# Transposing k's column maxima and spreading them over the partitions: the tensor engine's transpose mode in place of float32 products with the identity

## The chip, the cores and the metric

The kernel runs on one core of a Trainium2 chip. The metric is the device time of one execution in microseconds. The kernel before takes 540.25 us (median of three runs, 539.28 to 540.41).

## What is computed

For batch 8, 8 heads, 576 positions and head width 64, a linear attention feeds a gated MLP over 512 channels. The part that the change touches is the softmax of k over the positions (`axis=2`), which takes the maximum of each of k's columns first. Cut from the reference:

```python
    k_s = k - np.max(k, axis=2, keepdims=True)
    k_s = np.exp(k_s)
    k_s = k_s / (np.sum(k_s, axis=2, keepdims=True) + 1e-09)
    kv = np.einsum('bhsd,bhse->bhde', k_s, v)
    return np.einsum('bhsd,bhde->bhse', q_s, kv).astype(np.float32)
    ...
    h = x @ w_in
    ...
    v_s = np.einsum('ts,bsd->btd', w_sg, v_n) + b_sg[None, :, None]
    gated = u * v_s
    return (x + gated @ w_out).astype(np.float32)
```

The MLP has a tanh GELU behind `w_in` and a layer norm over one half of its channels ahead of `w_sg`.

## The kernel before, in words

All 8 batch elements (b) go through one core. Work is written as small steps, and a table (`PLAN`, lines 28 to 125) says in which order the steps are recorded; each engine then runs its instructions in that order. PE's matmuls all stand at line 330 (the helper `mm`), the other engines' at line 142 (the class `InOrder`), so in the profile steps are told apart by the names of their tiles.

The large products (`hv_mm`, `hu_mm`, `sg_mm`, `out_mm`: x by `wi`, normed v by `ws`, the gate by `wo`) are each split into three products of a high and a low part in the reduced float32 form (fp32r), with 288 or 512 moving columns. In the attention, k, q and v of one half h of the heads (4 heads, 256 columns) are handled at once, so every k step runs 16 times (b, h). The k steps in their order:

- `load_k`: DMA of k into tile `kk` (128 partitions of positions, 5 x 256).
- `k_max` (DVE, tile `km`): maximum over the five position tiles; 128 partitions x 256 columns are left.
- `kt_mm` (PE, line 354): for each 128 columns a matmul with the 128x128 block of `km` as the weights and `eye`, the float32 identity, as the moving operand. The result in PSUM is the block transposed.
- `k_top` (DVE, tile `kt`): maximum along the free axis of the PSUM tile; one number for each column of k is left, one a partition.
- `kb_mm` (PE, line 364): the column of `kt` is read as the weights, repeated 128 times (`broadcast_to([P, P])`), and again multiplied with `eye`: every partition of the PSUM tile gets all 256 maxima.
- `k_sub` (DVE, writes `kk` from `kk` and the PSUM tile), `k_exp` (ACT), `kv_mm` (PE, float32, `vv,kk` in the profile), which sums over the positions.

`kt_mm`, `kb_mm`, `kv_mm` and `hv_mm` take turns on two one-bank PSUM tiles (`ps1`); the other products use three two-bank tiles (`ps2`). `kt_mm` and `kb_mm` stand in PLAN among the large products, so that k's steps run beside them. A float32 matmul of the program becomes two weight loads and two matmuls in the profile (`eye,km` x64 for 16 `kt_mm` of two calls); an fp32r one becomes one of each.

Of the kernel before, what the change touches and what calls it, by code (L numbers as in the profile page):

```python
# [15 lines left out]
P = 128  # L16
# [155 lines left out]
def gmlp_kernel(ctx: ExitStack, tc: tile.TileContext, q, k, v, w_in, g_ln, w_sg, b_sg, w_out, identity, out):  # L172
# [7 lines left out]
    def sb(name, shape, dt=F32, tag=None):  # L180
        return pool.tile(shape, dt, name=name, tag=tag or name)

    def slots(name, n, shape, dt=F32):
        return Slots(pool, name, n, shape, dt)
# [6 lines left out]
    eye = sb("eye", [P, P])  # L191
# [9 lines left out]
    km_s = slots("km", 2, [P, 512])  # L201
# [11 lines left out]
    def bank(tiles, *key):  # L213

        count[id(tiles)] = n = count.get(id(tiles), -1) + 1
        st[key] = tiles[n % len(tiles)]
        return st[key]
# [111 lines left out]
    def mm(*args, **kw):  # L329
        tc.keep_in_program_order(nc.tensor.matmul(*args, **kw))  # L330
# [18 lines left out]
    def columns(ps):  # L349
        return ps[:, 0:256].rearrange("p (a n) -> p a n", a=2)  # L350

    def kt_mm(b, h):

        ps = columns(bank(ps1, "kt", b, h))
        for a in range(2):
            mm(ps[:, a], km_s(b, h)[:, a * P:(a + 1) * P], eye, start=True, stop=True)

    def k_top(b, h):

# [2 lines left out]
    def kb_mm(b, h):  # L362

        ps, top = columns(bank(ps1, "kb", b, h)), kt_s(b, h)
        for a in range(2):
            mm(ps[:, a], top[:, a:a + 1].broadcast_to([P, P]), eye, start=True, stop=True)

    def k_sub(b, h):
        kk = kk_s(b, h, at=h)
# [288 lines left out]
```

## Time and profile before

| | |
|---|---|
| runs | 540.41, 539.28, 540.25 us |
| profiled execution | 539.78 us, its span from the first to the last instruction 538.0 us |
| PE matmul busy | 491.1 us (91%), 3888 matmuls and 3888 weight loads |
| DVE busy | 379.3 us (71%) |
| ACT busy | 249.7 us (46%) |
| POOL busy | 125.8 us (23%) |
| chain that ended last | PE 85%, DVE 9%, DMA 3% |
| mean granted TensorE clock | 0.983 |

A group of instructions is named by what it writes and reads, `ps<-eye,km` being a matmul into PSUM with the identity moving and `km` as the weights. A matmul's duration is longer than its share of a stream, since matmuls are pipelined; what one costs in a stream is the distance between starts. Idle time of an engine is given with the instruction that ended it.

### The profile page before, as it was taken

How to read it: one execution, taken by the hardware profiler on the slowest of the kernel's cores; microseconds unless marked ns; L12 is line 12 of the kernel's file. 1: busy time of each engine (PE TensorE's matmuls, PEld its weight loads, DVE VectorE, ACT ScalarE, POOL GpSimd, SP SyncE). 2: the span in 40 equal slices, each digit the busy share in tenths (PEclk: the TensorE clock that was granted, in tenths of full speed). 3: DMA queues.
4: the chain of work that ended last, by engine and by line, in shares of the span. 5: the costliest groups of instructions: out<-in, count | busy, mean ns of one | idle time of the engine just before them, and what ended most of it. 6: DMA issues, size and time to landing. Idle time of an engine off the chain costs nothing.

```text
span 538.0 us, 9392 instructions
## 1 busy us (share of the span) xinstructions
PE 491.1 (91%) x3888; PEld 453.6 (84%) x3888; DVE 379.3 (71%) x646; ACT 249.7 (46%) x425; POOL 125.8 (23%) x104
## 2 busy tenths in 40 slices
PE   0251999999999999999999999999999999999997
PEld 0140877999998988999999988999989988999997
DVE  8999799999879788876756877965363566243114
ACT  4474685648375355762564264751154144131110
POOL 0324312331332003251211313530111002012211
PEclk9995899999999999999999999999999999999999
DMA  9991062013421620121412332023100100001002
GB/s 323 368 390 79 3 211 97 1 46 121 148 105 32 256 90 1 44 99 67 127 40 100 111 121 88 1 99 122 68 1 0 67 23 1 1 0 67 23 2 88
DMA packets 19054, 48.87 MB, mean 91 GB/s; under 512 B 1602, under 2 KB 8132, under 8 KB 19012
## 3 DMA queue, kind: packets, MB, share of 16 engines
q1 hardware_dynamic: 19012, 48.28, 25.2%
q8 instruction: 30, 0.49, 0.4%
q14 instruction: 12, 0.10, 0.1%
HBM read 38.83 MB, written 9.44 MB: 90 GB/s over the span
## 4 chain that ended last, share of the span: by engine, by line
PE 85%; DVE 9%; DMA 3%; issue 1%; ACT 1%; POOL 0%; SPq 0%; DVEq 0%; POOLq 0%
PE ps L330 85%; DVE km L142 2%; DMA qq<-q 1%; DVE ot_i L142 1%; DMA kk<-k 1%; DVE kk L142 1%; DVE wi_l L142 1%; DVE qm L142 1%; DVE qd L142 1%; DVE qq L142 1%; DVE ulow L142 1%; DVE qt L142 0%; ACT qe L142 0%; POOL qq L142 0%; DVE u L142 0%
## 5 line engine op out<-in xcount | busy, mean ns | idle before, releaser
L142 POOL TENSOR_TENSOR rs<-ve,half 128x1 f32<-128x1 f32 x36 | 30.6, 850 | 158.5 <-DVE ve L142 158.5
L142 DVE TENSOR_TENSOR u<-ps,u 128x576 f32<-128x576 f32 x32 | 24.0, 751 | 54.2 <-PE ps L330 54.1
L330 PE MATMUL ps<-gh,wo_h 128*128 128x288 f32 x256 | 56.2, 298 | 0.0
L330 PE MATMUL ps<-ulow,wo_h 128*128 128x288 f32 x256 | 55.6, 296 | 0.5 <-DVE ulow L142 0.5
L330 PE MATMUL ps<-ws_h,vnh 128*128 128x288 f32 x256 | 55.8, 299 | 0.0
L330 PE MATMUL ps<-gh,wo_l 128*128 128x288 f32 x256 | 55.3, 294 | 0.0
L330 PE MATMUL ps<-ws_l,vnh 128*128 128x288 f32 x256 | 54.8, 295 | 0.0
L330 PE MATMUL ps<-ws_h,vnl 128*128 128x288 f32 x256 | 54.8, 295 | 0.0
L142 ACT ACT_TABLE_LOAD x38 | 48.8, 1283 | 8.1 <-PE ps L330 5.2
L142 ACT ACTIVATE v<-ps 128x512 f32<-128x512 f32 x36 | 21.5, 598 | 64.3 <-PE ps L330 63.0
L142 ACT CAST gh<-u 128x576 fp32r<-128x576 f32 x32 | 21.5, 672 | 58.7 <-DVE u L142 58.4
L142 DVE TENSOR_TENSOR o<-ps,x_h 128x576 f32<-128x576 f32 (+1 forms) x33 | 24.2, 735 | 31.5 <-PE ps L330 31.4
L142 POOL TENSOR_TENSOR qq<-qq,qd 128x576 f32<-128x576 f32 x22 | 28.2, 1295 | 69.6 <-DVE qd L142 46.5
L142 POOL TENSOR_TENSOR ulow<-u,gh 128x576 fp32r<-128x576 f32 x16 | 23.8, 1488 | 82.3 <-ACT gh L142 64.0
L330 PEld LDWEIGHTS ps<-gh,wo_h 128*128 128x128 f32 x256 | 41.4, 188 | 1.3 <-issue 0.4
L330 PEld LDWEIGHTS ps<-ulow,wo_h 128*128 128x128 f32 x256 | 41.2, 188 | 1.1 <-DVE ulow L142 1.0
L330 PEld LDWEIGHTS ps<-ws_h,vnh 128*128 128x128 f32 x256 | 41.4, 189 | 0.4
L330 PE MATMUL ps<-wi_h,x_h 128*128 128x512 f32 x144 | 40.6, 404 | 0.8 <-DVE kk L142 0.8
L330 PEld LDWEIGHTS ps<-ws_l,vnh 128*128 128x128 f32 x256 | 41.3, 188 | 0.0
L330 PEld LDWEIGHTS ps<-ws_h,vnl 128*128 128x128 f32 x256 | 41.3, 188 | 0.0
L330 PEld LDWEIGHTS ps<-gh,wo_l 128*128 128x128 f32 x256 | 41.2, 188 | 0.0
L330 PE MATMUL ps<-x_h,wi_h 128*128 128x288 f32 x256 | 40.9, 303 | 0.0
(90 smaller groups left out, 1063.5 us busy)
## 6 DMA issues: line engine op xcount, KB each, us to landing
vv<-v SPq DMA_DIRECT2D x16, 650.0 KB, 6.6
kk<-k SPq DMA_DIRECT2D x16, 640.0 KB, 4.8
qq<-q SPq DMA_DIRECT2D x16, 576.0 KB, 3.6
out<-o SPq DMA_DIRECT2D x31, 288.0 KB, 2.1
ghws<-w_sg SPq DMA_DIRECT2D x5, 320.0 KB, 7.9
raw_vnh<-w_in SPq DMA_DIRECT2D x2, 512.0 KB, 9.5
raw_wo_l<-w_in SPq DMA_DIRECT2D x2, 512.0 KB, 8.5
raw_vnl<-w_in SPq DMA_DIRECT2D x2, 512.0 KB, 8.8
```

The costliest lines, as they stand in the source:

```text
L142: ins = op(*args, **kw)
L330: tc.keep_in_program_order(nc.tensor.matmul(*args, **kw))
```

## The change

Both calls with the identity get `is_transpose=True`. The order of the steps, the operands, the tiles and all other engines' instructions stay as they are.

```diff
@@ kt_mm
         ps = columns(bank(ps1, "kt", b, h))
         for a in range(2):
-            mm(ps[:, a], km_s(b, h)[:, a * P:(a + 1) * P], eye, start=True, stop=True)
+            mm(ps[:, a], km_s(b, h)[:, a * P:(a + 1) * P], eye, is_transpose=True, start=True, stop=True)
@@ kb_mm
         ps, top = columns(bank(ps1, "kb", b, h)), kt_s(b, h)
         for a in range(2):
-            mm(ps[:, a], top[:, a:a + 1].broadcast_to([P, P]), eye, start=True, stop=True)
+            mm(ps[:, a], top[:, a:a + 1].broadcast_to([P, P]), eye, is_transpose=True, start=True, stop=True)
```

In the compiled program each of the 64 calls (16 x 2 steps x 2) is now one weight load and one matmul where it was two of each: 3824 matmuls and 3824 weight loads in place of 3888 and 3888.

## Rows read from the trace of the kernel before

**Rows 1.** The page, busy tenths of 40 slices (13.45 us each), and the granted clock.
```profile
PE   0251999999999999999999999999999999999997
DVE  8999799999879788876756877965363566243114
PEclk9995899999999999999999999999999999999999
```
**Rows 2.** Busy time by stretch: stretch, length, PE, weight loads, DVE, ACT, POOL, clock.
```profile
57.00:90.00 33.00, 32.11 (x258) 26.69 (x258) 29.86 (x63) 23.02 (x39) 10.11 (x10) 0.98 0.39 127
230.00:300.00 70.00, 70.00 (x606) 66.34 (x604) 47.48 (x74) 34.25 (x48) 15.62 (x11) 1.00 0.25 87
410.00:538.00 128.00, 124.06 (x924) 116.97 (x922) 53.32 (x97) 31.07 (x49) 21.02 (x18) 0.99 0.08 29
```
**Rows 3.** The chain of waits in order of time: start, length, what.
```profile
72.02 72.34 PE ps L330 x620
...
144.37 6.56 DMA kk<-k
...
169.93 351.18 PE ps L330 x2768
```
**Rows 4.** Matmuls with the identity by stretch: stretch, length, PE busy (count).
```profile
57.00:144.30 87.30, 5.85 (x40) 0.99 0.25 83
144.30:170.00 25.70, 1.21 (x8) 1.00 0.29 104
170.00:230.00 60.00, 1.92 (x12) 1.00 0.25 95
230.00:410.00 180.00, 8.30 (x52) 1.00 0.22 78
```
**Rows 5.** Timeline of PE, 101 to 104.5 us: start, length of the merged piece, count.
```profile
101.99 0.60 PE L330 MATMUL ps<-eye,km 128*128 128x128 f32 x4
102.43 0.61 PE L330 MATMUL ps<-eye,kt 128*128 128x128 f32 x4
102.80 0.51 PE L330 MATMUL ps<-ws_h,vnh 128*128 128x288 f32 x2
```
**Rows 6.** Timeline of PE, 347 to 350.5 us, beside matmuls of another array form (128*64).
```profile
347.91 0.61 PE L330 MATMUL ps<-eye,km 128*128 128x128 f32 x4
348.45 1.39 PE L330 MATMUL ps<-vv,kk 128*64 128x65 f32 x40
349.76 0.71 PE L330 MATMUL ps<-eye,kt 128*128 128x128 f32 x4
350.23 0.51 PE L330 MATMUL ps<-ws_h,vnh 128*128 128x288 f32 x2
```
**Rows 7.** Timeline of PE, 22 to 33 us: the first steps of k.
```profile
22.74 2.08 PE L330 MATMUL ps<-eye,km 128*128 128x128 f32 x8 [22.74 <-DVE km L142]
24.61 1.09 PE L330 MATMUL ps<-eye,kt 128*128 128x128 f32 x4
```
**Rows 8.** Timeline of DVE, 22 to 33 us: its idle time before k_top and k_sub.
```profile
24.00 0.42 DVE L142 TENSOR_REDUCE kt<-ps 128x2 f32<-128x256 f32 x1 [0.26 <-PE ps L330]
24.86 0.42 DVE L142 TENSOR_REDUCE kt<-ps 128x2 f32<-128x256 f32 x1 [0.43 <-PE ps L330]
...
32.32 1.49 DVE L142 TENSOR_TENSOR kk<-kk,ps 128x1280 f32<-128x1280 f32 x1 [0.40 <-PE ps L330]
```
**Rows 9.** DVE's waits in 60 to 90 us: us in total, times, longest.
```profile
DVE kt L142 <- PE ps L330: 2.1, 2, 1.5
```
**Rows 10.** Timelines of PE around 55 and 73 us: the same eight matmuls.
```profile
54.89 2.29 PE L330 MATMUL ps<-x_h,wi_h 128*128 128x288 f32 x8
56.98 1.95 PE L330 MATMUL ps<-x_h,wi_l 128*128 128x288 f32 x8
...
73.33 1.34 PE L330 MATMUL ps<-x_h,wi_h 128*128 128x288 f32 x8
74.50 1.23 PE L330 MATMUL ps<-x_h,wi_l 128*128 128x288 f32 x8
```

## The prediction

> **What bounds the kernel now.** I read the slices of the page first [rows 1]: from about 54 us to the end PE is busy nine tenths or more, and DVE is nearly as full up to about 140 us, then ever less. The stretches [rows 2] put numbers on that: from 57 to 90 us DVE works 29.86 of 33.00 us, from 230 to 300 us only 47.48 of 70.00, and PE is full in both. The chain of waits [rows 3] says the same: PE alone carries it from 72.02 to 144.36 us, then it runs through a load of k at 144.37 us and what follows from it on the other engines to 169.93 us, and from there 351.18 us on PE alone. So there are three stages: a start up to about 57 us that DVE sets, a stretch to about 230 us in which PE and DVE end each other's waits, and the rest, which is PE's own. A microsecond taken from PE is worth a whole one in the last stage, and less in the middle.
>
> **What the identity products cost.** They are 128 of PE's matmuls, 64 for turning the maxima and 64 for spreading them, four to a step (two calls of two). Matmuls overlap, so the cost is the distance between starts: the four of one step take from 101.99 to 102.43 us, 0.44 us [rows 5], 0.11 us each. Of the 32 steps 28 lie behind 57 us, by their counts over four [rows 4]: ten up to 144.3 us (40), two up to 170 (8), three up to 230 (12), thirteen up to 410 (52). The other four stand in the start.
>
> **What a transposed call will cost.** Each becomes one weight load and one matmul. No row shows the mode, so I bound it. *Upper end without a switch of form:* each matmul left costs what it costs now, 0.11 us, so a step takes 0.22 us and saves 0.22. *Lower end:* a float32 matmul streams its columns twice, as the kv products show: 40 of them, in side-by-side pairs of 65 columns, take 348.45 to 349.76 us [rows 6], 1.31 / 20 = 0.066 us for 130 column times. A transposed matmul that streams its 128 columns once would cost 0.065 us, a step 0.13, and save 0.31. Weight loads don't forbid it there: each matmul of the pair has one of its own, of 64 columns, inside those 0.066 us. I take 0.31, because a transposition has one value to hand on per column and no halves to multiply, and keep 0.22 for the range.
>
> The row that is nearest, then, gives 0.31. The Trainium skill, page TensorE: Matmul & The Clock Gate, section Terms, calls the transpose mode four times as fast for float32; an estimate from that is 0.44 / 4 = 0.11 us a step, 0.33 saved, and the sum below would be 7.5 in place of 7.1 us. No run here shows it yet.
>
> **The start.** There the products run at half the pace: eight from 22.74 to 24.61 us are 1.87 us, 0.23 each [rows 7]. DVE waits for them three times, 0.26 and 0.43 us before its two reductions and 0.40 us before the second subtraction [rows 8]. With half the matmuls or fewer these waits go, 1.09 us, and no more, since DVE is then held by its own work. DVE carries the chain from there to PE's restart at 52.78 us, so I count 1.1 us; the ends are 0.26 (one wait only) and 1.1.
>
> **57 to 230 us.** Here DVE has little idle time to give up: of the 3.1 us in 57 to 90 [rows 2], 2.1 are waits for a turned block [rows 9], which the change does shorten. Of the thirteen steps (ten and three) I count half, 13 x 0.31 / 2 = 2.0 us; the ends are nothing and all, 4.0. The two steps in the DVE part of the chain, 144 to 170 us, count nothing: PE would only wait longer at 169.93 us for what DVE has not finished.
>
> **From 230 us on.** Thirteen steps count in full, 13 x 0.31 = 4.0 us. What lets them count is DVE's slack, 22.5 us of the 70 from 230 us on and 74.7 of the last 128 [rows 2]: it can follow a PE that is a few microseconds early. What is late next there is still PE.
>
> **The sum:** 1.1 + 2.0 + 4.0 = 7.1 us. DVE's, ACT's and POOL's instructions, all DMAs and PSUM's turns are the same, so nothing else has a cost. Against the profiled execution, 539.78 us (span 538.0 and 1.8 around it), that is 532.7; the median of the runs is 0.5 us higher, so 540.25 - 7.1 = 533.1 us. Everything passed on would be 1.1 + 28 x 0.31 = 9.8, 530.5 us; nothing passed on in the middle, 5.1, 535.1 us.
>
> **The rivals.**
>
> *Half the gain.* The matmul that is left still streams twice, 0.22 us saved a step: 1.1 + 13 x 0.22 / 2 + 13 x 0.22 = 5.4 us, 534.9 us. For it: the float32 columns are read as two halves now. The same number comes out if one pass is enough, but entering the mode costs what entering the full array form from the halved one costs, 0.10 us (0.47 us from 349.76 to 350.23 [rows 6] against 0.37 [rows 5]): 0.31 - 0.10 = 0.21 a step.
>
> *The gain goes to switching.* If the mode is a form of its own, PE pays on entering (0.10) and on leaving: 0.54 us from 347.91 to 348.45 [rows 6] against 0.37, 0.17 more. A step then saves 0.31 - 0.27 = 0.04 us, 19.5 steps 0.8 us, and with half of the start 539.0 us, hardly to be told from no change. Against it: the tile form in the rows stays 128*128.
>
> *Slower.* Two passes and both switches: 0.22 - 0.27 = -0.05 us a step. If all 28 steps pass that on and the start gains nothing, it is 1.4 us, 541.7 us. It decides as soon as switching costs over 0.22 us a step. The Trainium skill, page TensorEngine Tiling (Array Packing), section Key Properties, says that changing the tiling mode drains the engine; the trace agrees at its changes of form, with the 0.10 and 0.17 us above, and shows nothing of the transpose mode.
>
> *The clock falls.* Around 55 us eight products start 2.09 us ahead of the next eight, around 73 us 1.17 us [rows 10]; the granted clock is 5 tenths in the slice from 40 to 54 us, the 1.2 GHz level, and 8 in the next [rows 1], after PE had stood still. These eight alone lose 0.92 us by it. If transposing looked like standing still, a lapse three times as long as they are would cost about 3 us; three such lapses would turn the gain into a loss of 2, 542 us. Against it: PE is full on both sides of every step behind 57 us, and a step is 0.13 us of it. The Trainium skill, page TensorE: Matmul & The Clock Gate, Part 4, says that transposes don't count as busy for the clock. By this rule alone the time would not change, unless such lapses come.
>
> *It doesn't do what it says.* One matmul in the mode could take as long as the two that it replaces; then 540.25 us.
>
> **How the numbers follow.** The forecast, one pass without a switch, 0.48; half the gain 0.28; gain gone to switching 0.10; slower 0.06; clock 0.04; no effect 0.04. Two tenths of a per cent, 1.1 us, is about what a measurement can tell from no change, so faster means under 539.2 us. Faster: 0.48 + 0.28 + half of the switching case, 0.81; same: the other half and no effect with a little of the slower case, 0.10; slower 0.09. The range takes in the forecast with both ends (530.5 to 535.1), half the gain with its own (1.1 + 2.9 without the middle, 536.3), and reaches to 538.0 for partly paid switches: some 0.8.
>
> **What would show it.** Right: 32 + 32 rows of matmuls with the identity, not 128; 0.13 us, not 0.44, from the turning to the spreading step where they stand back to back; the waits of DVE for `ps` at 24.0, 24.9 and 32.3 us gone; PE still over nine tenths after 57 us, with its busy time some 9 us less or the matmuls behind closer. Half: 0.22 us there. Switching: an extra 0.1 us or more at the first matmul behind a transposed one. Clock: a slice under 9 after 60 us. The prediction is wrong in its middle if PE's idle time for DVE between 57 and 230 us grows by more than 2 us, and wrong in its last stage if the stretch from 230 us on is not shorter by about 4.

## The result, and the profile after

The changed kernel takes 534.22 us (median of six runs, 533.78 to 534.75) where the kernel before, in six runs beside it, takes 539.25 us: a ratio of 0.9905, 95% interval 0.989 to 0.9921. A second comparison further down gives 0.9887 (0.9872 to 0.9903). So it is faster by 5 to 6 us; the forecast was 7.1 us saved and 533.1 us, the range 530.5 to 538.0. The profiled execution is 533.9 us with a span of 532.0.

Lines from the page of the changed kernel: busy time, two of the rows of slices that answer to [rows 1], and the chain that ended last.

```profile
PE 484.2 (91%) x3824; PEld 444.3 (84%) x3824; DVE 378.7 (71%) x646; ACT 249.5 (47%) x425; POOL 126.1 (24%) x104
...
PE   0151999999999999999999999999999999999997
...
PEclk9999999999999999999999999999999999999999
...
PE 74%; DVE 17%; issue 3%; DMA 2%; ACT 2%; POOL 1%; SPq 0%; POOLq 0%; DVEq 0%; ACTq 0%
```

PE is as full as before from the fifth slice on. Its busy time is 6.9 us less. What is new is the chain: DVE carries 17% of it, where it carried 9%.

The timeline of PE at the place of [rows 5], and below it at the place of [rows 6]:

```profile
99.96 0.38 PE L330 MATMUL ps<-eye,km 128*128 128x128 f32 x2
100.18 0.38 PE L330 MATMUL ps<-eye,kt 128*128 128x128 f32 x2
100.31 0.51 PE L330 MATMUL ps<-ws_h,vnh 128*128 128x288 f32 x2
100.66 0.43 PE L330 MATMUL ps<-ws_h,vnl 128*128 128x288 f32 x2
...
343.50 0.38 PE L330 MATMUL ps<-eye,km 128*128 128x128 f32 x2
343.81 1.39 PE L330 MATMUL ps<-vv,kk 128*64 128x65 f32 x40
345.12 0.43 PE L330 MATMUL ps<-eye,kt 128*128 128x128 f32 x2
345.31 0.52 PE L330 MATMUL ps<-ws_h,vnh 128*128 128x288 f32 x2
```

Two matmuls a step now, and 0.22 us from the turning to the spreading step (99.96 to 100.18) where it was 0.44. One call costs 0.11 us, as one of its two matmuls did before: the number of matmuls halved, the price of one did not change. There is no cost of a switch either. To the next full-form product it is 0.13 us (100.18 to 100.31, before 0.37), and the distance behind that is 0.35 us as before (100.31 to 100.66). In front of the kv products it is 0.31 us where it was 0.54, behind them 0.19 where it was 0.47. So a step gives back 0.23 us, and up to 0.28 next to a product of another array form.

The first steps of k, on PE [rows 7] and on DVE [rows 8]:

```profile
22.62 1.11 PE L330 MATMUL ps<-eye,km 128*128 128x128 f32 x4 [22.62 <-DVE km L142]
24.01 0.69 PE L330 MATMUL ps<-eye,kt 128*128 128x128 f32 x2 [0.28 <-DVE kt L142]
```
```profile
23.54 0.74 DVE L142 TENSOR_REDUCE kt<-ps 128x2 f32<-128x256 f32 x2
24.66 0.78 DVE L142 STREAM_TRANSPOSE qt<-qq 128x576 f32<-128x576 f32 x1 [0.38 <-POOL qq L142]
25.37 1.45 DVE L142 TENSOR_TENSOR kk<-kk,ps 128x1280 f32<-128x1280 f32 x1
...
31.31 1.48 DVE L142 TENSOR_TENSOR kk<-kk,ps 128x1280 f32<-128x1280 f32 x1
```

DVE's three waits for PE are gone: its two reductions run back to back, and the second subtraction starts at 31.31 us, 1.01 earlier. Of that, 0.12 us was there before any changed step (22.62 against 22.74 us). And DVE has a new wait, 0.38 us for POOL at 24.66 us, where before it had none at this instruction (25.20 us). The chain of waits of the changed kernel tells what became of the middle [rows 3]:

```profile
51.75 13.47 PE ps L330 x76
...
70.21 1.40 PE ps L330 x40
71.68 5.03 DMA kk<-k
...
106.96 1.47 DVE kk L142
...
122.06 0.68 DVE ulow L142
122.78 17.90 PE ps L330 x132
...
167.85 347.34 PE ps L330 x2736
```

Before, PE alone carried it from 72.02 to 144.36 us. Now DVE carries most of it from 71.68 to 122.78 us. A list of PE's own waits from 57 to 230 us agrees: 0.8 and 0.3 us in two waits before, 1.1 us in all, and 2.8 us after the change, 2.3 of them for DVE:

```profile
PE ps L330 <- DVE ulow L142: 1.0, 2, 0.7
PE ps L330 <- DVE kk L142: 1.0, 1, 1.0
PE ps L330 <- ACT gh L142: 0.5, 1, 0.5
PE ps L330 <- DVE kt L142: 0.3, 1, 0.3
```

Where the time comes from is read from three places that all traces have in common: the first product of `x_h` by `wi_h`, and two runs of kv products (the seventh and eighth; us from the span's start, from the timelines of PE):

| kernel | `x_h` product | kv, 7th run | kv, 8th run | end of span |
|---|---|---|---|---|
| before | 54.89 | 171.80 | 235.34 | 538.0 |
| changed | 53.86 | 169.70 | 232.54 | 532.0 |
| ahead by | 1.03 | 2.10 | 2.80 | 6.0 |

The last stage shows best: from the 7th kv products on, sixteen steps bring 3.9 us, 0.24 each. The start shows 1.0 us; of that some 0.2 us is the scatter of single traces, since kernels with an unchanged start are ahead by 0.17 and 0.18 us at this place too (table in section 2). In between lie twelve steps that freed 2.7 us of PE's time, and the lead grew by 1.1 us there; 0.2 of these are not the steps' but the clock's, which rose sooner within the `x_h` products (last section).

### The profile page after: what moved, and what is told of

It reads as the page before. It is cut to its first block, busy times and chain, and to the rows that moved or that the text cites. A ratio compares the mean times of both kernels' runs of the same rounds, so it can differ in the third digit from the quotient of the medians.

```text
span 532.0 us, 9264 instructions
## 1 busy us (share of the span) xinstructions
PE 484.2 (91%) x3824; PEld 444.3 (84%) x3824; DVE 378.7 (71%) x646; ACT 249.5 (47%) x425; POOL 126.1 (24%) x104
## 4 chain that ended last, share of the span: by engine, by line
PE 74%; DVE 17%; issue 3%; DMA 2%; ACT 2%; POOL 1%; SPq 0%; POOLq 0%; DVEq 0%; ACTq 0%
PE ps L330 74%; DVE km L142 2%; DVE ot_i L142 2%; DMA qq<-q 1%; DVE qm L142 1%; DVE qd L142 1%; DVE kk L142 1%; DVE v L142 1%; POOL qq L142 1%; DMA kk<-k 1%; DVE qq L142 1%; DVE s L142 1%; DVE x_l L142 1%; DVE wi_l L142 1%; DVE ulow L142 1%
```

## The experiments

**1. What one call costs (two probes).** The changed kernel, with twelve extra matmuls of another form ahead of a turning step in each of five batch elements; the step overwrites what they wrote. The first probe:

```diff
+        m, e = km_s(b, h), eye
+        for n in range(12 if h == 0 and b >= 3 else 0):
+            if b == 3:
+                mm(ps[:, 0], m[:, 0:P], e, is_transpose=True, start=True, stop=True)
+            elif b == 4:
+                mm(ps[:, 0, 0:64], m[0:64, 0:P], e[0:64, 0:64], is_transpose=True, start=True, stop=True)
+            elif b == 5:
+                mm(ps[:, 0, 0:64], m[:, 0:P], e[:, 0:64], start=True, stop=True)
...
         for a in range(2):
```

> The changed kernel with twelve extra matmuls ahead of the turning step of head half 0 in batch elements 3 to 7, each batch element with another form (they write the PSUM tile that the step then overwrites): 3 the transpose as it is, 4 the transpose of 64 partitions (identity 64x64, still 128 weight columns), 5 a float32 product with 64 identity columns, 6 with 32, 7 with all 128. To be read: the distance between starts. Theory: a transposed call costs 0.109 us because its 128 identity columns are still streamed twice. Then 3 gives 0.109 us, 4 about 0.055 to 0.06, 5 about 0.055 to 0.06 per matmul, 6 less again, 7 0.112. Rival: the weight load of 128 float32 columns takes 0.109 us and the stream is hidden in it. Then 3 to 7 all give about 0.11 us. Second rival, a fixed cost of the mode: 4 stays at 0.109 and 5 falls to 0.06.

Timeline of PE; a piece holds the twelve calls (a float32 product is two matmuls) and the step's own two transposes:

```profile
129.63 1.69 PE L330 MATMUL ps<-eye,km 128*128 128x128 f32 x14
131.08 0.51 PE L330 MATMUL ps<-gh,wo_h 128*128 128x288 f32 x2
...
193.48 1.32 PE L330 MATMUL ps<-eye,km 64*128 64x64 f32 x14
...
254.77 3.01 PE L330 MATMUL ps<-eye,km 128*128 128x64 f32 x26
257.54 0.51 PE L330 MATMUL ps<-gh,wo_h 128*128 128x288 f32 x2
...
300.57 3.01 PE L330 MATMUL ps<-eye,km 128*128 128x32 f32 x26
303.34 0.51 PE L330 MATMUL ps<-gh,wo_h 128*128 128x288 f32 x2
```

Fourteen transposes take 1.45 us, 0.109 from start to start. With 64 partitions the distance inside the piece is 0.062 us. The float32 products surprised: with 64 columns and with 32 columns alike 26 matmuls take 2.77 us, 0.112 us from start to start inside the piece, and the fifth form, with all 128 columns, has 0.112 us too. Neither my theory (0.06) nor the second rival holds for them: something that doesn't depend on the columns streamed takes 0.112 us, and the weight load of 128 columns is what these forms have in common. Whether the transposes were held by it too was open, since the one with 64 partitions was faster at the same 128 weight columns. The second probe changes weight columns and partitions:

```diff
+            if b == 3:
+                mm(ps[0:96, 0], m[:, 0:96], e, is_transpose=True, start=True, stop=True)
+            elif b == 4:
+                mm(ps[:, 0, 0:32], m[0:64, 0:P], e[0:64, 0:32], start=True, stop=True)
+            elif b == 5:
+                mm(ps[0:96, 0, 0:32], m[:, 0:96], e[:, 0:32], start=True, stop=True)
+            elif b == 6:
+                mm(ps[0:96, 0], m[:, 0:96], e, start=True, stop=True)
...
```

> As the first probe, the changed kernel with twelve extra matmuls in front of one turning step in each of batch elements 3 to 7 (the step then overwrites what they wrote): 3 transposes with 96 weight columns and all 128 identity columns, 4 float32 products of 64 partitions with 32 identity columns, 5 float32 products with 96 weight columns and 32 identity columns, 6 float32 products with 96 weight columns and 128 identity columns, 7 float32 products of 64 partitions with 64 identity columns. Theory now: the weight load of 128 columns of float32 sets the 0.109 us. Then 3 falls to about 0.082 us (96/128), 5 as well, and 6 stays at 0.11, as its columns are streamed twice. Rival: in the transpose the stream of 2 x 128 columns sets it; then 3 stays at 0.109. 4 and 7 tell whether the load of 64 partitions is shorter: 0.06 us if so, 0.11 if the weight columns alone count.

The timeline of PE, as above; a piece of 26 holds 24 matmuls of the form and the step's two transposes:

```profile
129.94 1.69 PE L330 MATMUL ps<-eye,km 128*96 128x128 f32 x14
131.38 0.51 PE L330 MATMUL ps<-gh,wo_h 128*128 128x288 f32 x2
...
193.88 3.23 PE L330 MATMUL ps<-eye,km 64*128 64x32 f32 x26
...
257.06 2.40 PE L330 MATMUL ps<-eye,km 128*96 128x32 f32 x26
259.22 0.51 PE L330 MATMUL ps<-gh,wo_h 128*128 128x288 f32 x2
...
302.24 3.00 PE L330 MATMUL ps<-eye,km 128*96 128x128 f32 x26
305.00 0.52 PE L330 MATMUL ps<-gh,wo_h 128*128 128x288 f32 x2
```

For the transposes the rival is right: with 96 weight columns a call still takes 0.109 us (14 in 1.44 us), so the load doesn't set it. What it scales with is the identity's side: 0.109 us at 128 and 0.062 at 64. For 128 columns 0.109 us is 256 column times at 2.4 GHz (0.107 us) and a little. A transpose that streams its float32 columns twice, like a product, fits both numbers. It is not shown beyond that: with the identity's side the probe halved its columns and its partitions together, so a cost that goes by partitions isn't excluded.

For float32 products there are two limits side by side. One is the load, 0.112 us for 128 weight columns and 0.085 for 96 (the distances inside the pieces), whether 128 partitions are loaded or 64 (0.112 in the second piece, and in the fifth form, 64 partitions with 64 identity columns). The other is the stream, 0.109 us with 96 weight columns and all 128 identity columns. The Trainium skill, page TensorE: Matmul & The Clock Gate, section LDWEIGHTS, has a load take its columns over 1.2 GHz, whatever the number of partitions; an estimate from that is 0.107 us for 128 columns and 0.080 for 96. The trace agrees to within 0.005 us for float32 products, and not for the transposes, where a call with 128 weight columns takes 0.062 us. By the Trainium skill, the same page, section Terms, the float32 transpose would be four times as fast; measured, a step went from 0.44 to 0.22 us, twice as fast, and the measurement decides.

**2. The stages by themselves.** Transpose mode in some batch elements alone; the same edit at both calls, here of the start:

```diff
-            mm(ps[:, a], km_s(b, h)[:, a * P:(a + 1) * P], eye, is_transpose=True, start=True, stop=True)
+            mm(ps[:, a], km_s(b, h)[:, a * P:(a + 1) * P], eye, is_transpose=b == 0, start=True, stop=True)
...
-            mm(ps[:, a], top[:, a:a + 1].broadcast_to([P, P]), eye, is_transpose=True, start=True, stop=True)
+            mm(ps[:, a], top[:, a:a + 1].broadcast_to([P, P]), eye, is_transpose=b == 0, start=True, stop=True)
```

with `1 <= b <= 3` for the middle, `b >= 4` for the late steps, and later `b <= 3`.

> Transpose mode in the four steps of batch element 0 alone. Theory: the start is DVE's and gains what DVE waited there, about 1.0 us (ratio 0.998). Rival: the early microsecond is swallowed by the middle, where PE and DVE hold each other; then 0 to 0.3 us.

> Transpose mode in the twelve steps of batch elements 1 to 3 alone (58 to 163 us). Theory: DVE holds this stretch, so of 12 x 0.225 = 2.7 us of PE time only about 1.0 us reaches the end (ratio 0.998). Rival: PE alone sets the time, all 2.7 us arrive (ratio 0.995).

> Transpose mode in the sixteen steps of batch elements 4 to 7 alone (187 us on). Theory: PE's own stage, all 16 x 0.225 = 3.6 us arrive (ratio 0.9933). Rival: ACT and DVE end PE's waits there too and half arrives, 1.8 us.

> Transpose mode in the sixteen steps of batch elements 0 to 3. If the start and the middle give up the same waiting time of DVE, the two together bring less than the sum of their traces (1.57 + 1.51 us at the end of the span): about 2.1 us, which is what the changed kernel's trace is ahead at 170 us (ratio 0.996). If they are independent: 3.1 us (ratio 0.994).

> Transpose mode in batch element 0 alone, once more, since its first comparison left 0.4 us (-0.05 to 0.9) where its trace is 1.57 us shorter than the trace of before. If the trace is typical: 1 to 1.6 us; if the trace was its fastest execution: 0.4 us.

| transpose mode in | steps | ratio, 95% interval | us gained | ahead at `x_h`, kv 7th, end (one trace) |
|---|---|---|---|---|
| start | 4 | 0.9992 (0.9983 to 1.0001) | 0.4 | 0.99, 1.56, 1.6 |
| start, again | 4 | 0.9982 (0.9973 to 0.9992) | 0.9 | 0.71, 0.86, 0.9 |
| middle | 12 | 0.9985 (0.9976 to 0.9994) | 0.9 | 0.18, 1.49, 1.5 |
| start and middle | 16 | 0.9970 (0.9958 to 0.9981) | 1.7 | 0.81, 1.59, 1.6 |
| late | 16 | 0.9934 (0.9921 to 0.9946) | 3.6 | 0.17, -0.14, 3.7 |

The late steps give what PE saves, 3.6 us from sixteen. The middle gives a third of its 2.7 us, as the theory had it, and its rival (all of it) lies outside the interval. The start is worth 0.4 to 0.9 us. Its first trace was of its shortest execution, and half a microsecond of its lead is the clock's: from the `x_h` to the `x_l` products it took 3.34 us, where the trace of before and the second trace of the start took 3.88. The second comparison doesn't decide between the two readings stated ahead of it, as its interval reaches from 0.4 to 1.5 us. Together start and middle bring 1.7 us. The sum of the two traces, 3.1 us, lies outside the interval, the sum of the timed parts (0.4 to 0.9, and 0.9) within it; so that they share the same waiting time is not shown. The parts sum to 4.9 to 5.4 us, the whole is 5.0 to 6.1.

**3. Other ways to one matmul a call.** A maximum that is rounded shifts a whole column of k alike, and the shift cancels in the softmax; so neither step needs float32. First the reduced float32 form, in ordinary products:

```diff
-    eye = sb("eye", [P, P])
+    eye_f, eye = sb("eye_f", [P, P]), sb("eye", [P, P], F32R)
...
-    km_s = slots("km", 2, [P, 512])
-    kt_s = slots("kt", 2, [P, 2])
+    km_s = slots("km", 2, [P, 512], F32R)
+    kt_s = slots("kt", 2, [P, 2], F32R)
...
-        Y.dma_start(out=eye, in_=identity)
+        Y.dma_start(out=eye_f, in_=identity)
+        G.tensor_copy(out=eye, in_=eye_f)
...
-            mm(ps[:, a], km_s(b, h)[:, a * P:(a + 1) * P], eye, is_transpose=True, start=True, stop=True)
+            mm(ps[:, a], km_s(b, h)[:, a * P:(a + 1) * P], eye, start=True, stop=True)
```

and then the same with bfloat16 in place of `F32R`.

> No transpose mode: the maxima (tiles km, kt) and the identity are kept in the reduced float32 form, and both steps are ordinary products, one weight load and one matmul a call (one POOL copy makes the identity; a maximum that is rounded shifts a whole column alike and cancels in the softmax). If a weight load of four-byte values takes 0.109 us whatever the mode, a step stays at 0.22 us and the time at the changed kernel's, 534 us (ratio 0.990). If reduced float32 loads faster, a step takes 0.13 us and the time is about 532 us (ratio 0.987).

> As the run before with the maxima and the identity in bfloat16, two bytes a value. Expected: weights of two bytes load faster and the columns are streamed once, 0.06 us a call, 0.12 us a step; 28 steps save 0.32 us each, in full from 170 us on (5.1), about a third before (1.3), and the start 0.4 to 1: about 7 us (ratio 0.987). Rival: PE is no longer what ends the stretch to 230 us, and the time stays at the changed kernel's 534 us.

> The changed kernel once more, beside the two runs before on the same chip: 534 us, ratio 0.990.

| kernel | us | ratio, 95% interval |
|---|---|---|
| reduced float32 products | 534.19 | 0.9899 (0.9882 to 0.9915) |
| bfloat16 products | 531.44 | 0.9850 (0.9835 to 0.9865) |
| changed kernel, again | 533.30 | 0.9887 (0.9872 to 0.9903) |

Timelines at the place of [rows 5]: PE with reduced float32, its weight loads (PEld), then PE with bfloat16:

```profile
100.15 0.33 PE L331 MATMUL ps<-eye,km 128*128 128x128 f32 x2
100.33 0.39 PE L331 MATMUL ps<-eye,kt 128*128 128x128 f32 x2
100.55 0.48 PE L331 MATMUL ps<-ws_h,vnh 128*128 128x288 f32 x2
...
100.26 0.30 PEld L331 LDWEIGHTS ps<-eye,kt 128*128 128x128 f32 x2
100.49 0.30 PEld L331 LDWEIGHTS ps<-ws_h,vnh 128*128 128x128 f32 x2
```
```profile
98.85 0.29 PE L332 MATMUL ps<-eye,km 128*128 128x128 bf16 x2
98.97 0.28 PE L332 MATMUL ps<-eye,kt 128*128 128x128 bf16 x2
99.06 0.51 PE L332 MATMUL ps<-ws_h,vnh 128*128 128x288 f32 x2
```

In reduced float32 the first two starts are 0.06 us apart, but the spreading step then takes 0.22 us (100.33 to 100.55) and the time stays at the changed kernel's: where two matmuls can start 0.06 us apart, the loads of 128 four-byte weights follow each other only every 0.11 us (two from 100.26 to 100.49). In bfloat16 neither limit is above 0.06 us a call: 0.12 us from 98.85 to 98.97, 0.09 us to the next product, and with that 531.44 us, about 8 us under the kernel before and 2 under the changed one, the fastest kernel here. The cheaper call need not be all of these 2 us. The middle one of DVE's three maxima takes 0.29 us with bfloat16 operands where it took 0.42, sixteen times; what that is worth was not measured by itself. And in its trace the full pace came sooner:

```profile
53.53 2.13 PE L332 MATMUL ps<-x_h,wi_h 128*128 128x288 f32 x8
...
56.57 1.22 PE L332 MATMUL ps<-x_l,wi_h 128*128 128x288 f32 x8
```

From the `x_h` to the `x_l` products it takes 3.04 us; the changed kernel takes 3.66 and, run again, 3.98. So 0.6 to 0.9 us of its lead in the traces lie there. From the 7th kv products to the end of the span, where PE alone sets the time, its trace gains 1.1 us on the changed kernel's, 0.07 us a step. Whether the clock rises sooner in each of its executions was not tested, nor was the transpose mode with bfloat16 operands.

## Why the prediction was right, and where it was not

- **The total:** by its saving the forecast is too high, 7.1 us against 5.0 and 6.1. That its 533.1 us is so near the measured 534.2 and 533.3 is in part luck: it was taken from a kernel before of 540.25 us, which in the four comparisons since takes 539.1 to 539.4.
- **The start, 1.1 us:** right in kind, somewhat too large. The three waits of DVE went, and PE's `x_h` product started 1.03 us earlier, some 0.85 of it by the change. The timed runs of the start alone give 0.4 to 0.9 us. The forecast held that DVE would then be bound by its own work alone; it waits 0.38 us for POOL instead.
- **57 to 230 us, half of thirteen steps, 2.0 us:** right in cause, and near in size. From the `x_h` product to the 8th kv products the trace gains 2.80 - 1.03 = 1.8 us, 1.6 without the clock's 0.2. The share of one half was assumed and not worked out from rows, so that it came out is luck. Three of the thirteen steps, those past 170 us, gave all they had (2.80 - 2.10 = 0.7); for the rest DVE holds PE, which the chain shows and the middle steps alone confirm. The forecast's bound for being wrong, PE's idle time for DVE growing by more than 2 us, was not reached: it grew from 1.1 to 2.3 us.
- **The last stage, 13 x 0.31 = 4.0 us:** right that all of it arrives, wrong in what a step frees. From the 8th kv products to the end the trace gains 3.2 us, 0.24 a step. By the forecast's own sign, a stretch not shorter by about 4 us, it is wrong here.
- **The step that failed** is the price of a transposed call: "I take 0.31, because a transposition has one value to hand on per column and no halves to multiply". The probes show a call that takes the time of two passes of its columns, 0.109 us where one pass was counted as 0.065. A step takes 0.22 us and frees 0.23, the end that the forecast kept for the range and for the rival "half the gain". That rival's 5.4 us saved is nearer to the measured 5.0 and 6.1 us than the forecast's 7.1, and its first reason, a matmul that still streams twice, is the one that fits the probes. Its second, a charge for entering the mode, is not there.
- **Two of the reasons on the way were not sound.** The kv products were read as telling that weight loads leave room; they load 64 columns, and the probe shows that a product's load of 128 takes 0.112 us. That the transposes escape this limit no row of before showed. And one pass over 128 columns was priced at 0.065 us from them; a bfloat16 call takes 0.06.
- **The other rivals:** no switching cost (0.13 us to the next product, and nothing more behind it), so neither "the gain goes to switching" nor "slower". No lapse of the clock either: from 60 us on the distances are those of before (0.35 us behind the step at 100 us), every slice stands at 9, and through fourteen transposes in a row in the probe's piece at 129.63 us no distance grows. Whether the clock would fall in a long stretch of transposes alone, steps of 0.22 us among full-time products don't show.

## What to carry to other kernels

Before a product with the identity is made cheaper, ask which of two limits holds it, the stream of its columns or the load of its weights: in float32 products both took 0.11 us here for 128 columns, so a change that takes away one leaves the other. If the values only need to be the same for everybody who uses them, as a softmax's maximum, two-byte operands lower both limits (0.06 us a call) and beat the float32 mode, here by 2 us, though perhaps not by the cheaper call alone. And count a microsecond saved on a full engine by stage: it was worth a whole one where only that engine was full, and a third where a second engine was nearly full beside it.

## What was not expected

- A float32 product with 32 moving columns takes as long as one with 128: 0.112 us a matmul, by its weight load. Shortening the identity would have brought nothing.
- A transpose of 64 partitions with 128 weight columns takes 0.062 us, less than the load of a float32 product of the same shape (0.112 us). So the mode's own load is faster at this shape; how fast was not measured, and neither was it at 128 partitions, where a call takes 0.109 us for whichever reason.
- The row of the granted clock can miss a stretch. In the changed kernel's page it stands at 9 throughout, yet its first eight `x_h` products take 2.09 us to the next start, the pace that before had a slice of 5. The changed kernel, and below it the last line of the same three before:

```profile
53.86 2.29 PE L330 MATMUL ps<-x_h,wi_h 128*128 128x288 f32 x8
55.95 1.74 PE L330 MATMUL ps<-x_h,wi_l 128*128 128x288 f32 x8
57.52 1.23 PE L330 MATMUL ps<-x_l,wi_h 128*128 128x288 f32 x8
...
58.77 1.22 PE L330 MATMUL ps<-x_l,wi_h 128*128 128x288 f32 x8
```

The next eight take 1.57 us (55.95 to 57.52), where eight take 1.17 at full pace [rows 10]: the full pace came in the middle of the second group. In the kernel before the second group takes 1.79 us (56.98 [rows 10] to 58.77), so the full pace came later there. That difference, 0.22 us, lies behind the `x_h` mark and counts in the table as a gain between it and the 7th kv products. It differs from trace to trace: from the `x_h` to the `x_l` products it is 3.88 us before, 3.66 and 3.98 in the changed kernel's two traces, 3.34 and 3.88 in those of the start alone, 3.38 in the middle's. Without it the lead of the middle's trace grows by 0.8 us between the marks and not by 1.3, which is near what the timed runs say (0.9). A difference of half a microsecond between two single traces should be looked for here first.
